# Fused attention and feed-forward: queries transposed a group sooner, half-width output tiles, one attention tile fewer

## The chip, the cores and the metric

The kernel runs on one core of a Trainium2 chip. A core has TensorE (PE, matmuls; its weight loads are listed apart as PEld), VectorE (DVE), ScalarE (ACT), GpSimd (POOL) and SyncE (SP), which run their own instruction streams and wait for each other through semaphores. SP, ACT and POOL also issue DMA transfers, which share 16 DMA engines. The metric is the device time of one execution in microseconds; lower is better. Everything below that has a time in it comes from the runs of the kernel, from the profile page of one profiled execution, or from queries of the trace of that execution. Line numbers (L309) are those of the kernel before the change.

## The reference

Two layers run one after the other on 8 batches, 12 heads, 448 positions and 64 dimensions per head:

```python
scores = (q @ k.transpose(0, 1, 3, 2)) / sqrt(64)
attn   = maximum(scores, 0) ** 2 / 448
x      = (attn @ v)  # heads side by side: 8 x 448 x 768
xn     = (x - mean(x)) / sqrt(var(x) + 1e-6) * g_ln
out    = x + maximum(xn @ w_ch1, 0) @ w_ch2   # w_ch1 768 x 3072, w_ch2 3072 x 768
```

There is no softmax: a score is squared after a Relu, so a product with the values needs no row sum. Inputs and output are float32; the kernel multiplies in bfloat16.

## The kernel before

**Groups.** The work of attention is cut into 24 groups (`groups`), three per batch, numbered 0 to 23; a group holds four heads (two rows `r` of two heads `hh`). For each group the kernel needs queries and keys transposed, with the head dimension on the partitions. In batches 0 and 1 PE makes these transposes. From group 6 on (`by_dma * G`) DMA transposes do, issued by SP: one for the keys of a group (`keys_dma`, L256, into a `kT` tile, of which there are three) and two for its queries (`queries_dma`, L261 and L262, into a `qT` tile, of which there are two). The sources come by loads that POOL issues (`load`, L120): the queries of a group into one of three fixed buffers (`qbuf`), its keys into one of three `k` tiles, its values into one of four.

**Scores and products.** For each of a group's seven key blocks `scores` does four small matmuls into a PSUM tile of the pool `ps_sc` (three tiles, L309), lets ACT write the Relu into a tile of the pool `apool` (ten tiles, L320) and DVE square it in place (L322). When the seven tiles of a group are there, `values` multiplies them with the values: 28 matmuls into another `ps_sc` tile (L339), in this order, where tile `i` and row `r` follow from `divmod(pr * J + j, 2)` with `J = 7`:

```python
for j in range(J):
    for hh in range(2):
        for pr in range(2):
            i, r = g["where"](pr, j)   # reads g["attn"][i]
```

DVE writes the product as `xT` and, times the norm's weight, as `xc`; POOL sums `xT` for the mean.

**Feed-forward.** `ffn1` multiplies `xc` with the first weights into `hT` (L525, 24 blocks of 448 columns per batch). `ffn2` multiplies `hT` with the second weights (L563): for each of 7 token tiles of 128 rows per pair of batches and each half of 384 columns, 24 matmuls into a bank of the pool `ps_mm` (two banks). The normalization's scale and the residual come afterwards: DVE multiplies the bank with `rstd` and adds `xtok`, the tokens of the pair transposed back by one long DMA transpose (`tokens`, L497), and writes the result into `o_sb` (L569). An `o_sb` tile has both halves, 768 columns; there are two. After the second half SP issues two stores of 64 rows each (L578). The very last token tile (`ffn2_last`) is cut into three pieces, one of 384 and two of 192 columns, each stored by itself from SP and from ACT (L599).

**The order.** The schedule is manual: each engine runs its instructions in the order in which the program text issues them, and the tile pools only add waits. Four pairs of batches pass through. While `ffn2` of one pair runs, the attention of the next pair is woven in (`interleave`): `attention` makes bundles of three score tiles, and after a bundle's item with `i` of 1 or 2 comes the product of the group before. After the last score tile of a group n comes a step, `transposed(n + 2)`, which issues on POOL the loads of keys n+5 and queries n+4 and on SP the two query transposes of n+2 and the key transpose of n+3. The stores of `ffn2` stand in the same SP queue. Between two such stages lie about 55 us of `ffn1` alone. Group 6 is transposed at the end of batch 1's attention, and group 7 by a step of its own right after `tokens(0)`.

The names that the change touches: `opool`, `apool`, the `qT` tiles, `keys_dma`, `queries_dma`, `transposed`, `item` in `attention`, `ffn2`, `ffn2_last`, and the call of `transposed` after `tokens(0)`.

Of the kernel before, what the change touches and what calls it, by code (L numbers as in the profile page):

```python
# [9 lines left out]
ALU = mybir.AluOpType  # L10
# [18 lines left out]
def kernel(  # L29
# [32 lines left out]
    J = S // HP  # L62
# [14 lines left out]
    wpool = ctx.enter_context(tc.tile_pool(name="w", bufs=1))  # L77
    io = ctx.enter_context(tc.tile_pool(name="io", bufs=4))
    tpool = ctx.enter_context(tc.tile_pool(name="t", bufs=2))
    apool = ctx.enter_context(tc.tile_pool(name="attn", bufs=10))  # L80
    xpool = ctx.enter_context(tc.tile_pool(name="x", bufs=1))
    xcpool = ctx.enter_context(tc.tile_pool(name="xc", bufs=2))
    xtpool = ctx.enter_context(tc.tile_pool(name="xt", bufs=1))
    hpool = ctx.enter_context(tc.tile_pool(name="h", bufs=1))
    opool = ctx.enter_context(tc.tile_pool(name="o", bufs=2))
    spool = ctx.enter_context(tc.tile_pool(name="stat", bufs=2))
    ps_sc = ctx.enter_context(tc.tile_pool(name="ps_sc", bufs=3, space=bass.MemoryType.PSUM))
    ps_mm = ctx.enter_context(tc.tile_pool(name="ps_mm", bufs=2, space=bass.MemoryType.PSUM))
# [19 lines left out]
    def load(n, names):  # L108
        if n >= len(groups):
            return  # L110
        b, m = groups[n]
        for name in names:
            if b == 1 and name != "v":
                o = (2 * m + "qk".index(name)) * 2 * S
                t = hold[:, o:o + 2 * S].rearrange("p (r s) -> p r s", r=2)
            elif name == "q":
                t = qbuf[m][:, D:D + 2 * S].rearrange("p (r s) -> p r s", r=2)
            else:
                t = io.tile([P, 2, S], bf16, tag=name, name=name + "_sb", bufs=4 if name == "v" else 3)
            nc.gpsimd.dma_start(t, srcs[name][b][:, m:NP:G, :])  # L120
            qkv[name, b, m] = t
# [90 lines left out]
    def transposes(b, m):  # L212


        if b == 0:
            o = 12 * 1024 + m * 2 * J * P
            sb = early[:, o:o + 2 * J * P].rearrange("p (i c) -> p i c", c=P)
        elif m:
            o = (m - 1) * 2 * J * P
            sb = hold[:, o:o + 2 * J * P].rearrange("p (i c) -> p i c", c=P)  # L220
        else:
            sb = tpool.tile([P, NB, P], bf16, tag="qT", name="qT_sb")
        dve, act = nc.vector.tensor_copy, nc.scalar.copy
        if (b, m) == (0, 0):

            cast(dve, "q", 0, 3)
            cast(act, "k", 0, 3)
            cast(act, "k", 3, J)
            idle(30)
            piece(sb, b, m, "q", ((dve, 0, 3),))  # L230
            idle(2)
            piece(sb, b, m, "k", ((dve, 0, 3), (dve, 3, J)))
            idle(3)
        elif b == 0:
# [15 lines left out]
    kts = {}  # L250

    def keys_dma(n):
        if n >= len(groups):
            return
        kts[n] = tpool.tile([P, J, P], bf16, tag="kT", name="kT_sb", bufs=3)
        nc.sync.dma_start_transpose(kts[n], qkv[("k",) + groups[n]].rearrange("p r s -> p (r s)"))  # L256

    def queries_dma(n):
        m, kt = groups[n][1], kts[n]
        qt = tpool.tile([P, NB, P], bf16, tag="qT", name="qT_sb")  # L260
        nc.sync.dma_start_transpose(qt[:, 0:2 * J + 1:2, :], qbuf[m][:, :])  # L261
        nc.sync.dma_start_transpose(qt[:, 1:2 * J:2, :], qbuf[m][:, D:D + 2 * S])  # L262

        def queries(i, r):
            o = (2 * i + r) // J * J + 1 - r
            return qt[:, o:o + J]
        st[groups[n]] = {
            "q": queries,
            "k": lambda i: kt[:, i],
            "where": lambda pr, j: divmod(pr * J + j, 2),  # L270
            "attn": []}
# [127 lines left out]
    def transposed(n):  # L399

        if groups[n][0] < by_dma:
            transposes(*groups[n])
            return


        if n == by_dma * G:
            keys_dma(n)
        else:
            if n == by_dma * G + 1:
                load(n + 2, "k")  # L410
            load(n + 3, "k")
            load(n + 2, "q")
        queries_dma(n)
        keys_dma(n + 1)

    def attention_block(b, blk):

# [36 lines left out]
    def attention(bs):  # L454

        lo, hi = bs[0] * G, (bs[-1] + 1) * G
        seq = [(n, i) for n in range(lo, hi) for i in range(J)]

        def item(n, i):
            scores(n, (i,), FULL)
            if i == J - 1 and n + 2 < len(groups):
                transposed(n + 2)

        def product(n):
            values(n, FULL)  # L470
            load(n + 4, "v")

        def bundle(items, at):
            for o, it in enumerate(items):
                item(*it)
                if o == at:
                    product(it[0] - 1)
        units, due = [], [[], []]
        for s in range(0, len(seq), 3):
            items = seq[s:s + 3]  # L480
            at = max((o for o, (n, i) in enumerate(items[:2]) if n > lo and i in (1, 2)), default=-1)
            units.append(lambda items=items, at=at: bundle(items, at))
# [67 lines left out]
        nc.scalar.activation(hT[pair][:, 0, o:o + w], one, ACTF.Relu)  # L550
        nc.scalar.activation(hT[pair][:, 1:3, o:o + w], two, ACTF.Relu)

    o_sb = {}

    def ffn2(pair, t, half, part, parts=4):
        if half == 0 and part == 0:
            o_sb[t] = opool.tile([P, d_model], fp32, tag="o", name="o_sb")
        if part == 0:
            o_sb["ps"] = ps_mm.tile([P, 512], fp32, tag="mm", name="o_ps")
        ps, cols = o_sb["ps"], slice(half * DH, (half + 1) * DH)  # L560
        n = K2 // parts
        for ki in range(part * n, (part + 1) * n):
            nc.tensor.matmul(  # L563
                ps[:, :DH], hT[pair][:, ki, t * P:(t + 1) * P], w2[:, ki, cols],
                start=(ki == 0), stop=(ki == K2 - 1))
        if part < parts - 1:
            return
        heads = slice(half * HP, (half + 1) * HP)
        nc.vector.scalar_tensor_tensor(  # L569
            o_sb[t][:, cols].rearrange("p (c d) -> p c d", d=D),  # L570
            ps[:, :DH].rearrange("p (c d) -> p c d", d=D),
            rstd[pair][:, t:t + 1], xtok[pair][:, :, t, heads],
            op0=ALU.mult, op1=ALU.add)
        if half == 1:
            for u in range(2):
                b, j = divmod(2 * t + u, J)
                rows = out[2 * pair + b].rearrange("(p j) d -> j p d", j=J)[j]
                nc.sync.dma_start(rows, o_sb[t][u * HP:(u + 1) * HP, :])  # L578

    def ffn2_last(pair, t):  # L580

        o = opool.tile([P, d_model], fp32, tag="o", name="o_sb")
        for half, lo, hi in ((0, 0, K1), (1, 0, G), (1, G, K1)):
            cols = slice(half * DH + lo * D, half * DH + hi * D)
            w = (hi - lo) * D
            ps = ps_mm.tile([P, 512], fp32, tag="mm", name="o_ps")
            for ki in range(K2):
                nc.tensor.matmul(  # L588
                    ps[:, :w], hT[pair][:, ki, t * P:(t + 1) * P], w2[:, ki, cols],
                    start=(ki == 0), stop=(ki == K2 - 1))  # L590
            nc.vector.scalar_tensor_tensor(  # L591
                o[:, cols].rearrange("p (c d) -> p c d", d=D),
                ps[:, :w].rearrange("p (c d) -> p c d", d=D),
                rstd[pair][:, t:t + 1], xtok[pair][:, lo:hi, t, half * HP:(half + 1) * HP],
                op0=ALU.mult, op1=ALU.add)
            for u, queue in enumerate((nc.sync, nc.scalar)):
                b, j = divmod(2 * t + u, J)
                rows = out[2 * pair + b].rearrange("(p j) d -> j p d", j=J)[j]
                queue.dma_start(rows[:, cols], o[u * HP:(u + 1) * HP, cols])  # L599

    def ffn1_units(b, blk=FULL):
        if blk == FULL:
# [35 lines left out]
    interleave(ffn1_units(1, BLK[1][0]), attention_block(1, BLK[1][1]), 3, 1)  # L638
    tokens(0)
    transposed(by_dma * G + 1)  # L640
    for unit in ffn1_units(1, BLK[1][1]):
        unit()
    statistics(0, 0)
# [42 lines left out]
```

## Time and profile before

| What | us |
|---|---|
| median of 3 runs (551.58 to 556.33) | 552.45 |
| profiled execution, its own time | 551.32 |
| its span, from the first to the last instruction | 549.5 |
| PE busy in the span | 538.7 |
| DVE, ACT, POOL busy | 266.0, 260.2, 109.2 |
| attention woven into output, first, second and third time | 102 to 176, 231 to 307, 362 to 436 |
| output of the last pair alone | 491 to 549.5 |

| Transfer | Issued by | Count | Issue to landing, median us |
|---|---|---|---|
| queries transposed, L261 and L262 | SP | 36 | 6.8 |
| keys transposed, L256 | SP | 18 | 5.2 |
| tokens transposed, L497 | SP | 4 | 12.3 |
| output, 192 KB each, L578 | SP | 54 | 3.6 |
| queries loaded, 224 KB each, L120 | POOL | 20 | 7.7 |
| keys loaded, 224 KB each, L120 | POOL | 20 | 7.2 |

A timeline row has the start, the length (of the whole run of instructions, where it merges several), the engine, the line, what is written and read, and in brackets the idle time before it and what ended that. A row with SPq is the issue of a transfer, not the transfer: SP can be held there while the DMA queues are full. The landing is the time of the semaphore update. In the rows by stage, the DMA share adds up the queues' packets over 16 engines and can pass 1 where two queues overlap.

### The profile page before, as it was taken

The page shows a single profiled execution, that of the slowest core. Times are in us where ns is not written, and L with a number is a line of the kernel's source. Part 1 is how long each engine was busy: PE and PEld are TensorE (multiplying, and loading weights), DVE is VectorE, ACT ScalarE, POOL GpSimd, SP SyncE. Part 2 cuts the span into 40 slices and gives each one's busy share as a digit, 9 for nine tenths or more (in the row PEclk, how much of TensorE's full clock was granted, in tenths as well). Part 3 has the DMA queues.
Part 4 walks back from the last instruction along what each step waited for, and adds up shares of the span by engine and source line. Part 5 has one row for each costly group of instructions (what it writes and reads, how often), then busy time and mean ns, then how long its engine had stood idle before and what let it go on. Part 6 is the DMA issues. An engine that isn't in the chain of part 4 may idle for free.

```text
span 549.5 us, 10988 instructions
## 1 busy us (share of the span) xinstructions
PE 538.7 (98%) x4734; PEld 318.3 (58%) x4734; DVE 266.0 (48%) x511; ACT 260.2 (47%) x424; POOL 109.2 (20%) x135
## 2 busy tenths in 40 slices
PE   7899999999999999999999999999999999999997
PEld 5687779655555555555555555555555555555655
DVE  4776753378886250057777532027687670001111
ACT  5776775455553444455545344445545244440000
POOL 7334102024426100003614400001230400000000
PEclk8999999999999999999999999999999999999999
DMA  9999999979999900028999960006941250001222
GB/s 188 207 204 208 210 194 148 117 116 162 164 176 127 212 2 1 0 59 144 123 142 160 173 124 1 0 1 91 170 102 30 60 100 0 1 0 30 58 57 58
DMA packets 107216, 56.62 MB, mean 103 GB/s; under 512 B 77216, under 2 KB 103712, under 8 KB 107168
## 3 DMA queue, kind: packets, MB, share of 16 engines
q1 hardware_dynamic: 79680, 29.77, 32.3%
q0 software_dynamic: 26976, 25.50, 31.7%
q8 instruction: 37, 0.61, 0.5%
q10 hardware_dynamic: 512, 0.66, 0.3%
q14 instruction: 11, 0.09, 0.1%
HBM read 51.91 MB, written 11.01 MB: 115 GB/s over the span
## 4 chain that ended last, share of the span: by engine, by line
PE 90%; DMA 8%; issue 0%; POOL 0%; DVE 0%; SPq 0%; POOLq 0%
PE o_ps L563 38%; PE h_ps L525 38%; PE sc_ps L309 6%; DMA w<-in_moe_w_ch_dram 5%; PE av_ps L339 5%; DMA qT_sb<-q_sb 2%; PE o_ps L588 1%; DMA q_sb<-in_q_dram 1%; PE h_ps L547 1%; PE sum_ps L387 1%; PE tr_ps L205 0%; POOL k_sb L120 0%; POOL q_sb L120 0%; DVE o_sb L591 0%; POOL identity masks.py:199 0%
## 5 line engine op out<-in xcount | busy, mean ns | idle before, releaser
L525 PE MATMUL h_ps<-xc_sb,w 128*128 128x448 bf16 (+2 forms) x1368 | 219.2, 318 | 0.6 <-DVE hT_sb L531 0.4
L563 PE MATMUL o_ps<-w,hT_sb 128*128 128x384 bf16 x1296 | 219.6, 326 | 0.0
L525 PEld LDWEIGHTS <-w 128*128 128x128 bf16 x1368 | 128.6, 98 | 86.9 <-issue 3.1
L563 PEld LDWEIGHTS <-hT_sb 128*128 128x128 bf16 x1296 | 123.1, 98 | 94.2 <-issue 16.0
L320 ACT ACTIVATE attn_sb<-sc_ps 128x896 bf16<-128x896 f32 (+4 forms) x150 | 126.4, 902 | 84.6 <-PE sc_ps L309 84.6
L533 ACT ACTIVATE hT_sb<-h_ps 128x448 bf16<-128x448 f32 (+2 forms) x212 | 102.5, 483 | 121.5 <-PE h_ps L525 121.1
L322 DVE TENSOR_TENSOR attn_sb<-attn_sb 128x896 bf16<-128x896 bf16 x126 | 81.5, 654 | 39.1 <-ACT attn_sb L320 38.2
L569 DVE SCALAR_TENSOR_TENSOR o_sb<-o_ps,rstd_sb,xtok_sb 128x384 f32<-128x384 f32 x54 | 33.0, 611 | 49.1 <-PE o_ps L563 48.7
L510 DVE RECIPROCAL rstd_sb<-rstd_sb 128x1 f32<-128x1 f32 (+1 forms) x10 | 1.7, 168 | 98.0 <-ACT rstd_sb L509 98.0
L504 DVE BATCH_NORM_STATS2 stats<-xtok_sb 128x6 f32<-128x384 bf16 x56 | 27.5, 533 | 32.7 <-DMA xtok_sb<-xT_sb 32.7
L370 POOL TENSOR_TENSOR part_sb<-part_sb,xT_sb 128x448 f32<-128x448 f32 x24 | 29.5, 1229 | 66.9 <-DVE xT_sb L346 59.3
L367 POOL TENSOR_TENSOR part_sb<-xT_sb 128x448 f32<-128x448 bf16 x6 | 6.6, 1106 | 168.6 <-DVE xT_sb L346 138.7
L393 DVE SCALAR_TENSOR_TENSOR xc_sb<-total_sb,g_mean,xc_sb 128x448 bf16<-128x448 f32 (+2 forms) x54 | 29.0, 605 | 21.2 <-ACT total_sb L391 21.2
L309 PE MATMUL sc_ps<-qT_sb,kT_sb 64*64 64x448 bf16 x504 | 34.7, 357 | 1.5 <-DMA qT_sb<-q_sb 1.5
L339 PE MATMUL av_ps<-attn_sb,v_sb 64*64 64x448 bf16 (+2 forms) x672 | 32.3, 327 | 0.0
L346 DVE TENSOR_SCALAR xT_sb<-av_ps 128x896 bf16<-128x896 f32 (+2 forms) x30 | 26.9, 900 | 9.4 <-PE av_ps L339 9.4
L352 DVE TENSOR_SCALAR xc_sb<-xT_sb,g_sb 128x448 bf16<-128x448 bf16 (+2 forms) x56 | 28.6, 558 | 1.0
L339 PEld LDWEIGHTS <-v_sb 64*64 64x64 bf16 x840 | 22.9, 107 | 10.6 <-issue 1.6
L120 POOL DMA_DIRECT2D k_sb<-in_k_dram x20 | 14.2, 713 | 47.0 <-DMA kT_sb<-k_sb 37.0
L309 PEld LDWEIGHTS <-kT_sb 64*64 64x64 bf16 x504 | 11.5, 105 | 18.5 <-issue 15.0
L120 POOL DMA_DIRECT2D v_sb<-in_v_dram x24 | 17.4, 729 | 21.7 <-PE av_ps L339 17.9
L320 ACT ACTIVATE early<-sc_ps 128x768 bf16<-128x768 f32 (+3 forms) x24 | 18.3, 827 | 2.7 <-PE sc_ps L309 2.5
(63 smaller groups left out, 196.1 us busy)
## 6 DMA issues: line engine op xcount, KB each, us to landing
out_dram<-o_sb SPq DMA_DIRECT2D x54, 192.0 KB, 3.6
v_sb<-in_v_dram POOLq DMA_DIRECT2D x24, 224.0 KB, 4.9
w<-in_moe_w_ch_dram POOLq DMA_DIRECT2D x12, 384.0 KB, 14.5
w<-in_moe_w_ch_dram POOLq DMA_DIRECT2D x4, 1152.0 KB, 20.0
q_sb<-in_q_dram POOLq DMA_DIRECT2D x20, 224.0 KB, 7.7
k_sb<-in_k_dram POOLq DMA_DIRECT2D x20, 224.0 KB, 7.2
hold_sb<-in_q_dram POOLq DMA_DIRECT2D x3, 224.0 KB, 11.9
hold_sb<-in_k_dram POOLq DMA_DIRECT2D x3, 224.0 KB, 11.1
```

Of the source, the lines that this page charges most:

```text
L120: nc.gpsimd.dma_start(t, srcs[name][b][:, m:NP:G, :])
L309: nc.tensor.matmul(ps[cols, r, o * w:(o + 1) * w], g["k"](i)[rows, cols], g["q"](i, r)[rows, blk[0]:sum(blk), cols], start=True, stop=True)
L320: nc.scalar.activation(a, ps[:, :, :len(slots) * w], ACTF.Relu)
L322: nc.vector.tensor_mul(a, a, a)
L339: nc.tensor.matmul(ps[cols, hh, :w], v_sb[rows, pr, j * D:(j + 1) * D], g["attn"][i][rows, r, :], start=(j == 0), stop=(j == J - 1))
L352: nc.vector.tensor_scalar_mul(xc[b][:, c, of(blk)], xT[b // 2][:, c, of(blk, b)], g_sb[:, c:c + 1])
L370: nc.gpsimd.tensor_add(part[b], part[b], x[:, c])
L393: nc.vector.scalar_tensor_tensor(xc[b][:, c, of(blk)], total, g_mean[:, c:c + 1], xc[b][:, c, of(blk)], op0=ALU.mult, op1=ALU.add)
L525: nc.tensor.matmul(ps[:, :w], w1[:, c, ni * P:(ni + 1) * P], xc[b][:, c, of(blk)], start=(c == 0), stop=(c == K1 - 1))
L533: nc.scalar.activation(hT[pair][:, ni, o:o + w], ps[:, :w], ACTF.Relu)
L563: nc.tensor.matmul(ps[:, :DH], hT[pair][:, ki, t * P:(t + 1) * P], w2[:, ki, cols], start=(ki == 0), stop=(ki == K2 - 1))
L569: nc.vector.scalar_tensor_tensor(o_sb[t][:, cols].rearrange("p (c d) -> p c d", d=D), ps[:, :DH].rearrange("p (c d) -> p c d", d=D), rstd[ ...
```

## The change

- The `qT` tiles get three buffers. The step after group n issues the transposes of group n+3, keys first, then the two for the queries; before, it issued the queries of n+2 and then the keys of n+3. The loads of a step are the keys and queries of one group, n+5; before, the keys of n+5 and the queries of n+4. There is one more call, for group 8, after `tokens(0)`; the keys of group 7 come after the token transpose, where they stood ahead of it.
- An output tile has 384 columns, and there are three of them; before, two of 768. Each half is stored after its own eviction, with two stores of 64 rows, so the stores are twice as many with half the bytes each. The last token tile goes through the same function, and its three pieces have a tile each.
- The pool of attention tiles has nine, before ten.

The instructions of PE, ACT and DVE and their order stay the same; what the waits name, and the queues of SP and POOL, change.

```diff
-    apool = ctx.enter_context(tc.tile_pool(name="attn", bufs=10))
+    apool = ctx.enter_context(tc.tile_pool(name="attn", bufs=9))
...
-    opool = ctx.enter_context(tc.tile_pool(name="o", bufs=2))
+    opool = ctx.enter_context(tc.tile_pool(name="o", bufs=3))
...
     def keys_dma(n):
-        if n >= len(groups):
-            return
...
     def queries_dma(n):
         m, kt = groups[n][1], kts[n]
-        qt = tpool.tile([P, NB, P], bf16, tag="qT", name="qT_sb")
+        qt = tpool.tile([P, NB, P], bf16, tag="qT", name="qT_sb", bufs=3)
...
-        if n == by_dma * G:
-            keys_dma(n)
-        else:
-            if n == by_dma * G + 1:
-                load(n + 2, "k")
-            load(n + 3, "k")
-            load(n + 2, "q")
+        if n > by_dma * G:
+            load(n + 2, "kq")
+        keys_dma(n)
         queries_dma(n)
-        keys_dma(n + 1)
...
         def item(n, i):
             scores(n, (i,), FULL)
-            if i == J - 1 and n + 2 < len(groups):
-                transposed(n + 2)
+            if i == J - 1 and n + 3 < len(groups):
+                transposed(n + 3)
...
         if part < parts - 1:
             return
-        heads = slice(half * HP, (half + 1) * HP)
-        nc.vector.scalar_tensor_tensor(
-            o_sb[t][:, cols].rearrange("p (c d) -> p c d", d=D),
-            ps[:, :DH].rearrange("p (c d) -> p c d", d=D),
-            rstd[pair][:, t:t + 1], xtok[pair][:, :, t, heads],
-            op0=ALU.mult, op1=ALU.add)
-        if half == 1:
-            for u in range(2):
-                b, j = divmod(2 * t + u, J)
-                rows = out[2 * pair + b].rearrange("(p j) d -> j p d", j=J)[j]
-                nc.sync.dma_start(rows, o_sb[t][u * HP:(u + 1) * HP, :])
+        finish(pair, t, half, 0, K1, ps, (nc.sync, nc.sync))
+
+    def finish(pair, t, half, lo, hi, ps, queues):
+
+        cols, w = slice(half * DH + lo * D, half * DH + hi * D), (hi - lo) * D
+        o = opool.tile([P, DH], fp32, tag="o", name="o_sb")
+        nc.vector.scalar_tensor_tensor(
+            o[:, :w].rearrange("p (c d) -> p c d", d=D),
+            ps[:, :w].rearrange("p (c d) -> p c d", d=D),
+            rstd[pair][:, t:t + 1], xtok[pair][:, lo:hi, t, half * HP:(half + 1) * HP],
+            op0=ALU.mult, op1=ALU.add)
+        for u, queue in enumerate(queues):
+            b, j = divmod(2 * t + u, J)
+            rows = out[2 * pair + b].rearrange("(p j) d -> j p d", j=J)[j]
+            queue.dma_start(rows[:, cols], o[u * HP:(u + 1) * HP, :w])
...
     tokens(0)
     transposed(by_dma * G + 1)
+    transposed(by_dma * G + 2)
```

More of the change, by code (lines that the diff above doesn't have):

```diff
@@ L221, in transposes @@
         else:
-            sb = tpool.tile([P, NB, P], bf16, tag="qT", name="qT_sb")
+            sb = tpool.tile([P, NB, P], bf16, tag="qT", name="qT_sb", bufs=3)
         dve, act = nc.vector.tensor_copy, nc.scalar.copy
@@ L551, in ffn1_head @@
         nc.scalar.activation(hT[pair][:, 1:3, o:o + w], two, ACTF.Relu)
-    o_sb = {}
+    acc = [None]
     def ffn2(pair, t, half, part, parts=4):
-        if half == 0 and part == 0:
-            o_sb[t] = opool.tile([P, d_model], fp32, tag="o", name="o_sb")
         if part == 0:
-            o_sb["ps"] = ps_mm.tile([P, 512], fp32, tag="mm", name="o_ps")
-        ps, cols = o_sb["ps"], slice(half * DH, (half + 1) * DH)
+            acc[0] = ps_mm.tile([P, 512], fp32, tag="mm", name="o_ps")
+        ps, cols = acc[0], slice(half * DH, (half + 1) * DH)
         n = K2 // parts
@@ L567, in ffn2 @@
             return
-        heads = slice(half * HP, (half + 1) * HP)
+        finish(pair, t, half, 0, K1, ps, (nc.sync, nc.sync))
+    def finish(pair, t, half, lo, hi, ps, queues):
+        cols, w = slice(half * DH + lo * D, half * DH + hi * D), (hi - lo) * D
+        o = opool.tile([P, DH], fp32, tag="o", name="o_sb")
         nc.vector.scalar_tensor_tensor(
-            o_sb[t][:, cols].rearrange("p (c d) -> p c d", d=D),
-            ps[:, :DH].rearrange("p (c d) -> p c d", d=D),
-            rstd[pair][:, t:t + 1], xtok[pair][:, :, t, heads],
+            o[:, :w].rearrange("p (c d) -> p c d", d=D),
+            ps[:, :w].rearrange("p (c d) -> p c d", d=D),
+            rstd[pair][:, t:t + 1], xtok[pair][:, lo:hi, t, half * HP:(half + 1) * HP],
             op0=ALU.mult, op1=ALU.add)
-        if half == 1:
-            for u in range(2):
-                b, j = divmod(2 * t + u, J)
-                rows = out[2 * pair + b].rearrange("(p j) d -> j p d", j=J)[j]
-                nc.sync.dma_start(rows, o_sb[t][u * HP:(u + 1) * HP, :])
+        for u, queue in enumerate(queues):
+            b, j = divmod(2 * t + u, J)
+            rows = out[2 * pair + b].rearrange("(p j) d -> j p d", j=J)[j]
+            queue.dma_start(rows[:, cols], o[u * HP:(u + 1) * HP, :w])
     def ffn2_last(pair, t):
-        o = opool.tile([P, d_model], fp32, tag="o", name="o_sb")
         for half, lo, hi in ((0, 0, K1), (1, 0, G), (1, G, K1)):
-            cols = slice(half * DH + lo * D, half * DH + hi * D)
-            w = (hi - lo) * D
+            cols, w = slice(half * DH + lo * D, half * DH + hi * D), (hi - lo) * D
             ps = ps_mm.tile([P, 512], fp32, tag="mm", name="o_ps")
@@ L590, in ffn2_last @@
                     start=(ki == 0), stop=(ki == K2 - 1))
-            nc.vector.scalar_tensor_tensor(
-                o[:, cols].rearrange("p (c d) -> p c d", d=D),
-                ps[:, :w].rearrange("p (c d) -> p c d", d=D),
-                rstd[pair][:, t:t + 1], xtok[pair][:, lo:hi, t, half * HP:(half + 1) * HP],
-                op0=ALU.mult, op1=ALU.add)
[L596 to L599, printed above, removed]
+            finish(pair, t, half, lo, hi, ps, (nc.sync, nc.scalar))
     def ffn1_units(b, blk=FULL):
```

## The prediction

> **What bounds the kernel now.** I read the page's busy line first, then the busy time by stage, then who waited for whom on TensorE (PE), then the timeline around the one wait found, and last the issue queue of SyncE (SP) there.
>
> ```profile
> span 549.5 us, 10988 instructions
> PE 538.7 (98%) x4734; PEld 318.3 (58%) x4734; DVE 266.0 (48%) x511; ACT 260.2 (47%) x424; POOL 109.2 (20%) x135
> ```
>
> By stage (length, then busy us of PE, PEld, DVE, ACT and POOL, PE clock, DMA share, GB/s):
>
> ```profile
> 0.00:42.00 42.00, 36.70 (x636) 28.39 (x638) 27.39 (x74) 28.80 (x51) 21.79 (x37) 0.96 1.18 200
> 102.00:176.00 74.00, 74.00 (x674) 40.12 (x673) 59.15 (x108) 37.76 (x50) 25.86 (x29) 1.00 0.96 147
> 231.00:307.00 76.00, 74.52 (x675) 40.36 (x674) 52.05 (x81) 37.18 (x45) 24.54 (x27) 1.00 0.88 124
> 362.00:436.00 74.00, 74.00 (x673) 40.12 (x672) 52.11 (x80) 36.93 (x45) 15.63 (x15) 1.00 0.45 78
> 491.00:549.50 58.50, 54.52 (x360) 34.22 (x357) 9.07 (x16) 0.63 (x2) 0.00 (x0) 1.00 0.19 48
> ```
>
> PE stands idle for 549.5 - 538.7 = 10.8 us: 5.3 at the start (weights still loading), 4.0 at the end (last eviction and store), and 1.48 between, all of it in the second attention stage, 231 to 307. The first and third attention stages have no idle time at all. So the change, which touches the attention and output stages, can win 1.5 us and not much more, and it loses only what it makes PE wait.
>
> The Trainium skill ("Trainium Kernel Development and Optimization", Performance Expectations) warns that matmul busy time is a bad measure, since matmuls overlap, and would have one look at weight loads, here 58%; by that a large reserve could hide in the 98%. The row decides otherwise: successive 384-column matmuls of L563 start 162.5 ns apart (124.009, 124.171, 124.334), and that page's 2.4 GHz makes 160 ns of 384 columns.
>
> The one wait, in the timeline:
>
> ```profile
> 263.55 2.32 SPq L261 DMA_TRANSPOSE qT_sb<-q_sb  x1
> 265.92 2.99 SPq L262 DMA_TRANSPOSE qT_sb<-q_sb  x1
> 269.01 4.86 SPq L256 DMA_TRANSPOSE kT_sb<-k_sb  x1
> ...
> 274.07 0.38 PE L309 MATMUL sc_ps<-qT_sb,kT_sb 64*64 64x448 bf16 x4
> ...
> 275.26 1.11 SPq L578 DMA_DIRECT2D out_dram<-o_sb  x2
> ...
> 275.94 0.57 PE L309 MATMUL sc_ps<-qT_sb,kT_sb 64*64 64x448 bf16 x8 [1.48 <-DMA qT_sb<-q_sb]
> ```
>
> Group 16's query transposes are issued at 263.55 and 265.92, after the last scores of group 14; the second lands at 275.80, 9.9 us later, and group 16 begins there instead of at 274.46. Set beside each group's first scores, the other landings are early, but some barely: group 9 by 1.5 us (134.65 against 136.19), group 10 by 0.9, group 17 by 0.3 (288.97 against 289.25). The groups come about 10 us apart, and the landings of query transposes range from 3.1 to 11.4 us: the lead of one group is just too short where the DMA share is near or over 1.
>
> **The change, part by part.**
>
> 1. *Queries a group sooner, with their keys.* The step after group n now issues keys and queries of n+3; before it issued queries of n+2 and keys of n+3. The number of transposes per step (three), of loads (one k, one q) and their order on the engines PE, ACT and DVE are the same. The lead of a query transpose grows by a group, some 10 us, so the 1.48 us goes: **-1.5**. What is late next? Keys have that lead already, and no wait for keys is in PE's list; the worst step above lasted from 263.55 to the keys' landing at 276.49, 13 us, where the new lead is 20. The third buffer is what allows it: queries n+3 overwrite those of n, whose scores have just been issued, as with two buffers before.
>
> On POOL the load of queries n+5 now waits for the transposes of n+2, issued a step before, as the load of keys did already; POOL spent 37 us in such key waits with nothing late for it, and the sums behind (L370) waited for DVE, not for POOL.
>
> At the start there is one more step: after the token transpose of pair 0 come keys and queries of 7, then of 8. Keys 7 used to be issued at 80.28, ahead of the token transpose, which holds SP from 85.68 to 97.13; now they come after. Queries 7 were issued from 97.13 to 104.23 and landed at 107.81; with 1.3 us of keys ahead, 109.1; group 7 begins at 113.2: 4 us to spare. Group 8 follows on SP to about 110, lands by about 116 (queries had a median of 6.8 us), and begins at 123.2. **0**; with the longest landing of any, 11.4 us from a start near 101, still 112.4 and 0. If this cover goes, PE waits once, for the excess.
>
> 2. *Half tiles out.* DVE's 57 evictions are the same instructions. 54 stores of 192 KB become 108 of 96 KB. SP gets 54 more issues of 0.53 us (the pairs take 1.11): 28.6 us over the span, 1.1 us per group. In the worst step SP has no idle time from 262.34 to 273.87, so the transposes behind can slip 1.1 us per step, over the four such steps (263 to 306) 4.4 us: less than the 10 us gained. The three half buffers give a store the time of three halves: half 0 evicted at 271.58 would be issued when SP is free, at 273.9 to 275, land by 281.5 (the stores' longest landing is 7.5 from issue), and its buffer is wanted at about 285. DVE doesn't wait; and behind DVE PE has a second o_ps bank, half a tile or 3.9 us of matmuls, more with scores between. **0**. The tail: the last pieces have the same sizes and queues as before (1.9 to 2.4 us to landing), and the buffer of the last was stored 7.8 us earlier. **0**.
>
> The Trainium skill speaks against this part ("DMA: Bandwidth & Descriptors", Rules for kernel authors: coalesce small transfers, under 64 KB they are mostly overhead; Anatomy of one DMA gives 2.0 us fixed plus bytes/436e3). By its formula alone, 54 more stores would be 108 us of fixed cost if nothing overlapped it. The trace's 96 and 48 KB stores at the end landed in 1.9 to 2.4 us, which agrees with the fixed part, but nothing waits there for a store except the program's end.
>
> 3. *Nine attention tiles.* Ten were alive where the product of group n-1 is issued after score tile 2 of group n (four times per pair: products of its groups 0, 1, 3, 4). Now the Relu of tile 2 must wait until the product has read tile 0 of the old group. The product runs over j outermost, then hh, then pr; tile 0 holds the blocks j=0 and j=1 of pr=0, so its last reader is the 7th of 28 matmuls. The places where two scores follow the product in the same bundle matter (products 0 and 3 of a pair; 6 in all), since the third then needs the scores' bank of tile 2:
>
> ```profile
> 283.75 0.38 PE L309 MATMUL sc_ps<-qT_sb,kT_sb 64*64 64x448 bf16 x4
> 283.96 1.49 PE L339 MATMUL av_ps<-attn_sb,v_sb 64*64 64x448 bf16 x28
> 284.18 0.92 ACT L320 ACTIVATE attn_sb<-sc_ps 128x896 bf16<-128x896 f32 x1 [2.67 <-PE sc_ps L309]
> ...
> 285.29 0.55 PE L309 MATMUL sc_ps<-qT_sb,kT_sb 64*64 64x448 bf16 x8
> ```
>
> The 7th matmul ends at 284.51 and the scores at 284.13: the Relu starts 0.38 us later, ends near 285.48 instead of 285.10, and tile 4's scores start at 285.48 now. With a handover of 0.05 us (scores' end 284.132 to Relu's start 284.184) PE loses about 0.05 us; with that of the two PE waits on ACT's L320 that the trace has (0.7 us in 2), 0.35. I take 0.1, nearer the direct handover: **+0.6** for six; bounds 0 and 2.1. In the other six places scores of tile 1 are still in ACT's queue until after the 7th matmul: 0. In batch 1's blocks at most eight tiles are alive: 0.
>
> **Sum**: -1.5 + 0 + 0 + 0.6 = -0.9 us. The profiled execution took 551.32 us (span 549.5, 1.8 around it), so **550.4**. The runs' median, 552.45, lies 1.1 above the profiled one; landings that were early by 0.3, 0.9 and 1.5 us may have been late in those, and this is what a longer lead also removes, so I stay at 550.4 and not at 551.5.
>
> **The rivals.**
>
> *A. The gain is eaten* (551.3 to 552.6). The handover costs 0.25 to 0.35 us in each of the six places, 1.5 to 2.1 us, or the transposes were not what made the runs differ. For: PE must be woken within 0.1 us. Against: the Relu starts 0.05 us behind its scores everywhere.
>
> *B. Slower: the Relu waits for the whole product.* If tile 0 is let go only when all 28 matmuls have ended (285.457), the Relu ends at 286.43 and tile 4's scores lose 0.95 us, six times 5.7, less the 1.5: +4.2, **555.5**. It decides from a release later than the 7th matmul by more than 0.1 us. Against: the order of reads above.
>
> *C. Slower: halves slow a full DMA queue.* 3,456 more packets at the hardware queue's mean (32.3% of 16 engines over 549.5 us for 79,680 packets: 36 ns) are 7.7 us of all sixteen engines, 2.8 of it in the 20 halves or so of the two dense stretches; if transposes are that much later and the lead doesn't cover it, -1.5 + 0.6 + 2.8: **553.2**. It decides only once a step's backlog passes 20 us.
>
> *D. A clean gain* (549.0 to 549.9): handover free, and nothing lost.
>
> **How the numbers follow.** Forecast (549.9 to 551.3) 0.50; A 0.19; B 0.08; C 0.08; D 0.10; B and C together, or a stall on SP that I don't see, beyond 558: 0.05. The range, 549.0 to 554.0, holds the forecast, A, D and C. A measurement here can tell about 1% from no change: faster than 546.9 would need half of all PE's idle time, 0.02; within 1% 0.91; above 558 0.07 (the 0.05, and a part of B).
>
> **What would show it.** Right: no wait of PE for qT_sb; the second attention stage full on PE at 75 to 76 us; in the six places a Relu that starts 0.8 us after its scores do, not 0.43 (283.75 to 284.18); PE busy near 538.7. Wrong: PE waiting for ACT's L320 by more than 0.1 us a place, DVE waiting for out_dram stores, PE waiting for kT_sb or qT_sb at 113 or 123 us, or a longer span with PE idle in the first or third attention stage, where there is none now.

## The result and the profile after

| Kernel | Runs | Median us | Lowest to highest us |
|---|---|---|---|
| before | 14 | 552.96 | 550.77 to 556.33 |
| after | 14 | 549.52 | 549.19 to 552.40 |

The ratio after to before is 0.9946, with a 95% interval of 0.9926 to 0.9966: faster by half a per cent, some 3 us. The forecast was 550.4 us, 0.9 below the profiled execution of before; the median came 1.8 below that execution. Which terms the other 0.9 us belong to is worked out below.

The first profiled execution of the changed kernel took 552.11 us and had a span of 550.3 us, more than the 549.5 of before. It isn't typical, and one row says why. This is the first stage of it (stretch, length, busy us of PE, PEld, DVE, ACT and POOL, granted clock, DMA share, GB/s):

```profile
0.00:42.00 42.00, 36.05 (x598) 27.43 (x599) 25.98 (x70) 27.29 (x47) 20.72 (x35) 0.88 1.18 199
```

The clock granted to PE was 0.88 in the first 42 us on average (it stood at 0.50 from 8 to 17 us), 0.96 in the profile of before. In a second profiled execution of the same kernel (run e3 below, 550.08 us) it was 1.00. The first place where the schedule has scores, product and scores in a row starts at 120.05 us in the one and at 118.04 in the other; these 2.0 us are the whole difference of the two executions (552.11 and 550.08). So the profile shown from here on is that of e3. Its page and its stages, in the order in which those of before were read:

```profile
span 548.3 us, 11108 instructions
PE 539.3 (98%) x4734; PEld 318.9 (58%) x4734; DVE 266.3 (49%) x511; ACT 260.1 (47%) x424; POOL 109.5 (20%) x135
...
q0 software_dynamic: 26976, 25.50, 31.8%
q1 hardware_dynamic: 84000, 29.77, 30.4%
```

```profile
0.00:42.00 42.00, 36.57 (x620) 28.38 (x622) 26.99 (x73) 28.47 (x50) 21.70 (x37) 1.00 1.18 200
102.00:176.00 74.00, 74.00 (x673) 40.18 (x672) 58.27 (x105) 38.09 (x51) 26.69 (x31) 1.00 0.99 152
231.00:307.00 76.00, 76.00 (x684) 41.28 (x682) 52.51 (x81) 37.22 (x45) 25.41 (x28) 1.00 0.84 128
362.00:436.00 74.00, 74.00 (x673) 40.12 (x671) 52.53 (x80) 36.49 (x43) 15.68 (x15) 1.00 0.38 72
491.00:548.30 57.30, 53.71 (x355) 33.67 (x352) 8.92 (x16) 0.00 (x0) 0.00 (x0) 1.00 0.20 49
```

The second attention stage, 74.52 us busy on PE before, is now full: 76.00 of 76. The list of waits has no line for `qT_sb` or `kT_sb`; as the three attention stages are full, none of what is left is in them, and DVE's one wait for a store is 0.2 us. Here are the first three lines of PE and that of DVE (us in total, times, longest):

```profile
PE tr_ps L205 <- DVE q_sb L158: 1.3, 1, 1.3
PE idle_ps L191 <- DVE ones L93: 1.1, 1, 1.1
PE sc_ps L307 <- ACT early L318: 1.0, 2, 0.7
...
DVE o_sb L565 <- DMA out_dram<-o_sb: 0.2, 1, 0.2
```

The timeline where group 16 waited before, SP first, then PE:

```profile
266.20 4.16 SPq L259 DMA_TRANSPOSE qT_sb<-q_sb  x1
270.41 2.89 SPq L260 DMA_TRANSPOSE qT_sb<-q_sb  x1
273.39 3.62 SPq L573 DMA_DIRECT2D out_dram<-o_sb  x4
```

```profile
274.73 0.76 PE L307 MATMUL sc_ps<-qT_sb,kT_sb 64*64 64x448 bf16 x12
```

The transposes are no faster to issue: SP still stands 7 us over a pair. But they are those of group 17; group 16's had landed at 263.70, 11 us ahead of its first scores. The bundle of twelve (four of group 15, eight of group 16), which was torn at 274.46 before, runs in one piece.

**A ledger by landmarks.** The matmuls of PE are the same in both kernels, so I set the profiles side by side by the starts of the six places of step 3, each the start of the four score matmuls just ahead of a product (283.75 in the prediction is the fourth):

| Stretch, us | before | after (e3) | difference |
|---|---|---|---|
| span's start to place 1 | 117.61 | 118.04 | +0.43 |
| place 1 to place 6 | 295.32 | 294.01 | -1.31 |
| place 6 to the last landing of a store | 135.19 | 135.26 | +0.07 |
| last landing to the span's end | 1.35 | 0.98 | -0.37 |
| span | 549.47 | 548.30 | -1.17 |

The first row varies by itself (117.3 to 118.7 in the profiles of the runs below, whatever the kernel). The second is the subject of the experiments: it holds both the wait and the cost of the nine tiles, and in a kernel with neither it is 293.65 (run e4). The last row I had not expected.

### The profile page after: what moved, and what is told of

It is laid out like the page before. It is cut to its first block, busy times and chain, and to the rows that moved or that the text cites. A ratio compares the mean times of both kernels' runs of the same rounds, so it can differ in the third digit from the quotient of the medians.

```text
span 550.3 us, 11108 instructions
## 1 busy us (share of the span) xinstructions
PE 540.8 (98%) x4734; PEld 320.1 (58%) x4734; DVE 266.4 (48%) x511; ACT 260.4 (47%) x424; POOL 109.5 (20%) x135
## 3 DMA queue, kind: packets, MB, share of 16 engines
q0 software_dynamic: 26976, 25.50, 32.3%
## 4 chain that ended last, share of the span: by engine, by line
PE 96%; DMA 2%; ACT 1%; DVE 1%; SPq 0%; issue 0%; DVEq 0%
PE o_ps L554 39%; PE h_ps L518 39%; PE sc_ps L307 7%; PE av_ps L337 6%; DMA g_sb<-in_moe_g_ln_dram 2%; PE o_ps L581 1%; PE h_ps L540 1%; PE sum_ps L385 1%; PE tr_ps L205 1%; ACT early L318 1%; DVE early L296 0%; ACT early L209 0%; SPq L177 0%; ACT xc_sb L348 0%; DVE early L209 0%; DVE hT_sb L524 0%
## 5 line engine op out<-in xcount | busy, mean ns | idle before, releaser
L565 DVE SCALAR_TENSOR_TENSOR o_sb<-o_ps,rstd_sb,xtok_sb 128x384 f32<-128x384 f32 (+1 forms) x57 | 34.4, 604 | 56.4 <-PE o_ps L554 49.8
L497 DVE BATCH_NORM_STATS2 stats<-xtok_sb 128x6 f32<-128x384 bf16 x56 | 27.5, 533 | 30.4 <-DMA xtok_sb<-xT_sb 30.4
L337 PE MATMUL av_ps<-attn_sb,v_sb 64*64 64x448 bf16 (+2 forms) x672 | 32.3, 327 | 0.0
L337 PEld LDWEIGHTS <-v_sb 64*64 64x64 bf16 x840 | 23.3, 109 | 10.3 <-issue 1.3
L307 PEld LDWEIGHTS <-kT_sb 64*64 64x64 bf16 x504 | 12.1, 105 | 17.6 <-issue 13.3
```

The costliest lines, as they stand in the source:

```text
L307: nc.tensor.matmul(ps[cols, r, o * w:(o + 1) * w], g["k"](i)[rows, cols], g["q"](i, r)[rows, blk[0]:sum(blk), cols], start=True, stop=True)
L337: nc.tensor.matmul(ps[cols, hh, :w], v_sb[rows, pr, j * D:(j + 1) * D], g["attn"][i][rows, r, :], start=(j == 0), stop=(j == J - 1))
L565: nc.vector.scalar_tensor_tensor(o[:, :w].rearrange("p (c d) -> p c d", d=D), ps[:, :w].rearrange("p (c d) -> p c d", d=D), rstd[pair][:, ...
```

## The experiments

Theory W: the gain is PE's wait for query transposes, which in many runs is longer than the 1.48 us of the profile, and the longer lead removes it. Rivals: K, the clock granted at the start; H, the half tiles do it. Then, for what makes the transposes late: F, the bytes that the stores put right ahead of them; S, the packet size of the stores; L, the loads that POOL issues in the same step. Each ratio is to the kernel before on the same chip.

### Set 1: which part, and is it the wait

Before: 551.53 us median of 28 runs (550.48 to 555.7).

**e1, no edit: the kernel before.**

> The kernel before, unchanged, for its spread and a second profile. Theory W (the gain is PE's wait for query transposes, which differs from one execution to the next): runs spread over several us, 550.8 to 556, at a TensorE clock that doesn't explain it (0.99 to 1.00), and in the profile the waits of TensorE for qT_sb add up to the run's time less about 549.5. Rival K (the runs differ by the granted clock at the start): times follow the clock, and the waits for qT_sb stay at 1.5 us.

Measured: 551.9 us (550.63 to 557.05, 12 runs), ratio 1.0008 (0.9981 to 1.0035). Its profile has the start at full clock and a longer wait than the first (the wait, then the first 42 us and the second attention stage):

```profile
PE sc_ps L309 <- DMA qT_sb<-q_sb: 2.6, 1, 2.6
```

```profile
0.00:42.00 42.00, 36.95 (x640) 28.80 (x642) 27.73 (x75) 28.80 (x51) 21.89 (x37) 1.00 1.18 200
231.00:307.00 76.00, 73.45 (x670) 39.68 (x668) 51.62 (x80) 37.06 (x45) 23.68 (x26) 1.00 0.83 122
```

The same kernel in another execution loses 2.55 us at the same group 16 where the first lost 1.48, and place 1 to place 6 takes 296.40 us. What the run has above 549.5, 2.75 us, is what this stretch lost against 293.65, as W asked. With the start at 1.00 it still takes 552.25 us, so K can't be the whole of it. The other half of the expectation, a spread that the clock doesn't explain, failed: the five of the 12 runs above 553 us have a mean granted clock of 0.991 to 0.995, the other seven (550.63 to 552.25 us) 0.999 or 1.000.

**e2, all of the change but the queries:** two `qT` buffers and the old step; half tiles and nine attention tiles stay.

```diff
-    opool = ctx.enter_context(tc.tile_pool(name="o", bufs=2))
+    opool = ctx.enter_context(tc.tile_pool(name="o", bufs=3))
-    apool = ctx.enter_context(tc.tile_pool(name="attn", bufs=10))
+    apool = ctx.enter_context(tc.tile_pool(name="attn", bufs=9))
     # ffn2, finish, ffn2_last as in the change; transposed() as before
```

> The changed kernel with the old step (queries of n+2, then keys of n+3, two query buffers, loads as before): half tiles and nine attention tiles stay. Theory W: no gain, within 0.3% of the kernel before (552 to 554), with waits for qT_sb in the profile. Rival H (half tiles bring the gain, by smaller bursts and by freeing SP sooner): 549.5, as the changed kernel.

Measured: 549.98 us (549.44 to 552.64, 12 runs), ratio 0.9964 (0.9946 to 0.9982). The wait at group 16 is still there, but 0.2 us long (place 1 to place 6 takes 294.45 us, 0.44 more than in the changed kernel):

```profile
PE sc_ps L309 <- DMA qT_sb<-q_sb: 0.2, 1, 0.2
```

That W alone makes the gain is refuted: without the lead, most of it is there. What is missing is the certainty: 4 of the 12 runs are above 550.5.

**e3, no edit: the changed kernel.**

> The changed kernel again, for a profile at full clock and its per-run clocks. Both theories: 549.3 to 549.8, no wait for qT_sb; runs at a mean clock near 0.991 come at 552. Rival K: the difference to the kernel before vanishes between runs of equal clock.

Measured: 549.51 us (549.36 to 550.1, 9 runs), ratio 0.9959 (0.9942 to 0.9976); the profile shown above.

**e4, before without the wait:** the scores of groups 6 to 23 read the key tile where they read the query tile. The query transposes are still issued, and nobody reads them.

```diff
         def queries(i, r):
             o = (2 * i + r) // J * J + 1 - r
-            return qt[:, o:o + J]
+            return kt[:, 0:J]
```

> The kernel before, in which the scores of groups 6 on read the transposed keys in place of the transposed queries, so the result is another; all query transposes are still issued, but nobody reads them. Full tiles and ten attention tiles. Theory W: TensorE loses no time in attention, 549.2 to 549.8, narrow spread, as the changed kernel less its handover cost (0 to 0.6). Rival H: stays at 552 to 553.5. Rival K: stays as spread out as the kernel before.

Measured: 549.63 us (549.12 to 552.24, 8 runs, the other seven up to 550.13), ratio 0.996 (0.994 to 0.998). Full tiles, ten attention tiles, all transfers, and only the wait gone: the gain is there. Place 1 to place 6 takes 293.65 us. Against this, before had lost 1.67 us in its first profile and 2.75 in e1, mostly the waits of 1.48 and 2.55 that the lists show. So the wait is what the change gains from, whichever part shortens it.

**The granted clocks of the runs.** In the 96 runs of before in the three sets, the median is 551.34 us at a mean clock of 0.999 and above (31 runs) and 553.97 below 0.995 (21 runs). In the runs of the changed kernel (the result, e3 and e12) it is 549.55 (21 runs) and 552.11 (3 runs). At equal clock some 1.8 us remain, near what e4 gives, so K isn't the gain. But K has a share in the spread: 36 of the 38 runs of before above 553 us have a clock below 0.999. Below 0.995 the changed kernel, which has no such wait, loses about as much. Between 0.995 and 0.998 it doesn't (549.48 in 11 runs, 551.57 at most), while 17 of 44 runs of before are above 553; why these are isn't shown. The 14 runs of before in the result have no clock on record, so how much of the 3.4 us between those two medians is the clock stays open.

### Set 2: why half tiles alone shorten it

Before: 552.77 us median of 33 runs (550.7 to 557.11).

**e5, before with half tiles alone** (`opool` with three half buffers, `ffn2` and `ffn2_last` through `finish`; ten attention tiles, old step).

```diff
-    opool = ctx.enter_context(tc.tile_pool(name="o", bufs=2))
+    opool = ctx.enter_context(tc.tile_pool(name="o", bufs=3))
     # ffn2, finish, ffn2_last as in the change
```

> The kernel before with half tiles alone (old step, two query buffers, ten attention tiles). After e2, theory F: half tiles let the queries land sooner, because half of a token tile's bytes have left before the step, so only 192 KB and not 384 KB stand right ahead of the query transposes in SP's queue. Then 549.2 to 550.2 median, with waits for qT_sb of 0 to 1 us; 0.4 under e2, the six handovers of 0.07 us that nine tiles cost. If instead the nine tiles had been what helped: 551.5 to 553.

Measured: 549.99 us (549.2 to 553.64, 11 runs), ratio 0.996 (0.9932 to 0.9987). Place 1 to place 6: 294.26, that is 0.61 lost in place of 1.67 to 2.75. Groups 16 and 17 begin 0.1 us after their second query transpose landed, so the margin is nil, and 4 of the 11 runs are above 550.8.

**e6, half tiles whose stores are all issued after the second half.**

```diff
+        held.append(store)
+        if half == 1 or queues[1] is nc.scalar:
+            for s in held:
+                s()
+            held.clear()
```

> Half tiles as in e5, but the stores of both halves are issued together after the second half, so that again 384 KB (in four stores) stand right ahead of the step. Theory F: the gain is gone, 551.5 to 553, waits for qT_sb of 1.5 us and more, in group 16. Rival S (the smaller size alone helps): as e5, 549.2 to 550.2.

Measured: 549.89 us (549.17 to 552.65, 11 runs), ratio 0.9949 (0.9923 to 0.9974), place 1 to place 6 294.35. PE still waits 0.5 us at group 16. This run was no test of F: a store of the first half waits only for its own half, and as SP had nothing in between, it issued them at 261.31 and 261.90, right behind the key transpose, as in e5 (260.44 and 261.04, with all of that schedule 1.3 us sooner). Run e9 holds them back.

**e7, before without the stores of the first three pairs** (42 of the 54 stores are left out, so most of the output isn't written).

```diff
-        if half == 1:
+        if half == 1 and pair == B // 2 - 1:
```

> The kernel before without the stores of the first three pairs (that part of the output is not written). Theory F: the queries land early enough everywhere, no wait for qT_sb, 549.2 to 549.8, and group 16's second query transpose lands 1.5 to 3 us earlier after the step's start than the 12.3 us of before. If stores have no part in it: the wait stays and so does 551.5 to 553.

Measured: 550.62 us (548.91 to 553.98, 10 runs), ratio 0.996 (0.9931 to 0.9988). With no store at all in the stage the wait is still 0.9 us:

```profile
PE sc_ps L309 <- DMA qT_sb<-q_sb: 0.9, 1, 0.9
```

So the stores aren't the cause: the second query transpose of group 16 still lands 11.5 us after its issue. They may be a part of the crowd, as the median is 2.15 us lower; of that, 0.37 is the shorter end of the program, described below. Nor is the kernel faster without these stores than with the half tiles (549.99). (Place 1 to place 6: 295.06; 0.33 of the loss lies at group 10 and 1.07 at group 16.)

**e8, before without the loads of queries, keys and values from group 9 on** (these groups compute with the rows of the batch before).

```diff
         for name in names:
+            if n >= 9:
+                qkv[name, b, m] = qkv[name, b - 1, m]
+                continue
```

> The kernel before without the loads of queries, keys and values from group 9 on (the three older groups' data are used again, so the result is another). If POOL's loads are the other half of the crowding: query transposes land 4 to 6 us after their issue in the stage from 231 to 307, not 6 to 12, no wait for qT_sb, 549.2 to 549.8. If the transposes are slow by themselves: landings stay near 7 us median and the wait stays.

Measured: 549.43 us (549.22 to 550.18, 10 runs), ratio 0.9943 (0.9918 to 0.9968), place 1 to place 6 293.65, no wait. The same step of SP:

```profile
263.21 1.30 SPq L264 DMA_TRANSPOSE qT_sb<-q_sb  x1
264.56 1.42 SPq L265 DMA_TRANSPOSE qT_sb<-q_sb  x1
266.02 1.85 SPq L259 DMA_TRANSPOSE kT_sb<-k_sb  x1
```

It takes SP 4.7 us where it took 10.3 (263.55 to 273.87), and the two query transposes land 5.2 and 4.7 us after their issue; before it was 11.3 and 9.9. The median landing of a query transpose is 3.6 us, before 6.8. What crowds the transposes are the loads beside them.

### Set 3: packets against bytes, and the loads themselves

Before: 551.57 us median of 35 runs (550.34 to 555.7).

**e9, full tiles stored with four stores of 64x384,** the second half's first, so that SP holds all four back until the tile is whole.

```diff
-                nc.sync.dma_start(rows, o_sb[t][u * HP:(u + 1) * HP, :])
+                nc.sync.dma_start(rows[:, DH:], o_sb[t][u * HP:(u + 1) * HP, DH:])
+            for u in range(2):
+                b, j = divmod(2 * t + u, J)
+                rows = out[2 * pair + b].rearrange("(p j) d -> j p d", j=J)[j]
+                nc.sync.dma_start(rows[:, :DH], o_sb[t][u * HP:(u + 1) * HP, :DH])
```

> Before with one edit: full output tiles, but four stores of 64x384 instead of two of 64x768, all issued after the second half, so the same 384 KB go out at once, in the packets of the half tiles. Theory F (half tiles help because the bytes ahead of group 16's transposes are half): as before, 551 to 553 us, and PE waits for group 16's query transposes by 1 us or more. Rival S (the smaller packets help): about 549.9 us and a wait below 0.5 us.

Measured: 550.33 us (549.14 to 552.45, 12 runs), ratio 0.997 (0.9948 to 0.9991). Place 1 to place 6: 294.22. The 0.57 us lost are at group 10; the second attention stage is full:

```profile
PE sc_ps L309 <- DMA qT_sb<-q_sb: 0.4, 1, 0.4
```

```profile
102.00:176.00 74.00, 73.63 (x671) 39.83 (x669) 58.84 (x107) 38.21 (x51) 24.94 (x28) 1.00 1.00 143
231.00:307.00 76.00, 76.00 (x685) 41.20 (x683) 52.52 (x81) 37.43 (x46) 25.17 (x28) 1.00 0.78 127
```

F's wait of 1 us at group 16 isn't there: the same bytes in one go, and most of the gain of the half tiles. S fits, but isn't shown. Of the 1.24 us between the medians 0.37 is the shorter end of the program, and at a clock of 0.999 and above they are 0.67 us apart (550.31 in 9 runs, 550.98 in 12). Something else moved besides the packets: the two further stores hold SP, so that the transposes go out 1.3 us later after the loads beside them (263.83 and 264.54) than before. And e7, with no store packets at all in the stage, kept the wait. Group 16's transposes, issued 2.2 us later than before (265.78), landed 8.1 and 7.4 us after their issue. How smaller store packets could let them by sooner isn't shown either: packets of transposes took 30 ns on average before and 29 here, no clear difference, while packets of stores went from 175 ns (3072 bytes) to about 89 (1536 bytes).

**e10, before with the loads later:** the loads of keys and queries that a step issues move on POOL's queue behind the first sum (L370) of the next product.

```diff
+    def late_loads(n):
+        if n >= by_dma * G:
+            load(n + 5, "k")
+            load(n + 4, "q")
...
+                if c == 2 * m:
+                    late_loads(b * G + m)
...
-            load(n + 3, "k")
-            load(n + 2, "q")
+                load(n + 3, "k")
+                load(n + 2, "q")
```

> Before with one edit: the loads of keys n+3 and queries n+2 that the step after group n issues on POOL's queue are issued later, behind the first sum of product n; the transposes of the step keep their place, two query buffers, full tiles and ten attention tiles stay. Theory L (the query transposes are late because the step's own loads move beside them): 549.1 to 549.8 us, hardly a spread, no wait of PE for qT_sb, and the query transposes of group 16 land within 7 us. Rival (whatever moves at that time crowds them, the loads no more than the rest): 551 to 553 us and a wait of 1 us or more at group 16, or a wait for kT_sb or qT_sb elsewhere.

Measured: 549.76 us (549.37 to 551.01, 12 runs), ratio 0.9958 (0.9939 to 0.9978), no wait for `qT_sb` or `kT_sb`, place 1 to place 6 293.65. The loads at group 16's transposes before:

```profile
262.15 0.74 POOL L120 DMA_DIRECT2D v_sb<-in_v_dram  x1
262.88 0.72 POOL L120 DMA_DIRECT2D k_sb<-in_k_dram  x1
263.59 0.73 POOL L120 DMA_DIRECT2D q_sb<-in_q_dram  x1
```

And here, with the transposes between loads at 261.59, 263.31 and then 270.60:

```profile
261.59 0.72 POOL L120 DMA_DIRECT2D q_sb<-in_q_dram  x1
...
263.31 0.74 POOL L120 DMA_DIRECT2D v_sb<-in_v_dram  x1
263.81 2.28 SPq L261 DMA_TRANSPOSE qT_sb<-q_sb  x1
...
266.14 2.92 SPq L262 DMA_TRANSPOSE qT_sb<-q_sb  x1
...
269.15 1.52 SPq L256 DMA_TRANSPOSE kT_sb<-k_sb  x1
270.60 0.74 POOL L120 DMA_DIRECT2D k_sb<-in_k_dram  x1
```

The two loads that stood at 262.88 and 263.59 have moved to 270.60 and later; those of the step before, moved likewise, now stand here, at 260.86 and 261.59, some 2 us sooner. So the crowd is spread out, not taken away. The transposes landed after 8.8 and 7.2 us, not within the 7 us expected, but 1.2 us ahead of their scores. So the wait goes with the full output tiles, two query buffers and ten attention tiles of before, by moving two loads. L holds in kind; the margin is thin.

**e11, the late loads and the half tiles together,** ten attention tiles, two query buffers (the edits of e5 and e10).

> The late loads of the run before together with the half tiles of the change, ten attention tiles and two query buffers kept. Theory L, with the ten tiles' cheaper handover (0.43 us over six places): 549.0 to 549.4 us, 0.2 to 0.5 below the changed kernel. Rival: as the changed kernel or behind it, 549.5 to 550, with a wait for qT_sb left in some runs.

**e12, no edit: the changed kernel beside it.**

> The changed kernel again, beside the three others on the same chip: 549.3 to 549.7 us by every theory, ratio to before 0.993 to 0.997.

Measured: e11 549.31 us (548.85 to 550.7, 12 runs), ratio 0.9952 (0.9932 to 0.9972); e12 549.62 us (549.23 to 552.47, 12 runs), ratio 0.9972 (0.9953 to 0.999). Place 1 to place 6: 293.65 and 294.01. The 0.36 us between them is what nine attention tiles cost in these five places. The medians differ by 0.31; as the two intervals overlap, the runs alone don't settle that e11 is faster, the trace says why it should be. Its margin at group 16 is 2.5 us, that of the changed kernel 12.1.

## Why the prediction was right, and where it was not

The time fell inside the range, but in the band of rival D (549.0 to 549.9), 0.9 below the forecast; D's reason, a handover at no cost, is not what happened. By the steps:

1. **Queries a group sooner, -1.5: right in kind, too small.** No wait for `qT_sb` is left in any profile of the changed kernel, and the margins of groups 7 to 17 are 7.8 us and more. The size was one execution's: place 1 to place 6 lost 1.67 us in that profile, 2.75 in e1, and with nothing else changed (e4) the medians differ by 1.9 us. The prediction said that the landings early by 0.3, 0.9 and 1.5 us could be late in other runs, and then stayed at the profile's number. It should have counted them: group 10, early by 0.9, was late in e7 and e9. The 1.1 us by which the runs' median lay above the profile was a possible sign, though the clock at the start moves runs as well. Runs of before up to 557 us remain without a profile; nearly all above 553 have a lowered clock, and how much of their excess is wait isn't shown.
2. **The step at the start, 0: right.** In e3 group 7's queries landed at 105.46, 8.1 us before its first scores, and group 8's at 110.74, 12.8 us before; I had allowed 109.1 and 116.
3. **Half tiles, 0: right that they cost nothing, wrong that they bring nothing.** Alone they gave 0.996 (e5). Two things were missed: half tiles shorten the wait by themselves (place 1 to place 6 loses 0.61 us in e5; 1.67 and 2.75 before), for a reason that e6, e7 and e9 leave open, and the program's end is 0.37 us shorter, of which more below. Since the longer lead removes the same wait, the two gains don't add up: e2 549.98, e5 549.99, the whole change 549.5. DVE's wait of 0.2 us is as good as the none I expected, and the two stores that SP issued at 273.39 and 273.99 had landed by 276.17 (allowed for such a pair: 281.5). The rule of the Trainium skill that spoke against this part ("DMA: Bandwidth & Descriptors", Rules for kernel authors: coalesce small transfers) puts its line at 64 KB, and the halves have 96 KB; its formula, in Anatomy of one DMA, is for transfers that GpSimd issues, and SP issues these. No cost of splitting showed here: the same bytes in twice the stores (e9) gave 0.997.
4. **Nine attention tiles, +0.6: right in kind, 0.43 in size.** The fourth place in the changed kernel, PE and then ACT:

```profile
282.73 0.38 PE L307 MATMUL sc_ps<-qT_sb,kT_sb 64*64 64x448 bf16 x4
282.94 1.50 PE L337 MATMUL av_ps<-attn_sb,v_sb 64*64 64x448 bf16 x28
284.26 0.62 PE L307 MATMUL sc_ps<-qT_sb,kT_sb 64*64 64x448 bf16 x8
284.82 0.34 PE L554 MATMUL o_ps<-w,hT_sb 128*128 128x384 bf16 x1
```

```profile
283.53 0.92 ACT L318 ACTIVATE attn_sb<-sc_ps 128x896 bf16<-128x896 f32 x1 [3.04 <-PE av_ps L337]
```

ACT's Relu now waits for the product (`av_ps`) and starts 0.80 us after the scores; I had said 0.8, against 0.43. The next `o_ps` matmul comes 2.09 us after the scores, 2.02 before: 0.07 us a place, in all six places alike, 0.43 together. In place of the 0.1 that I took, the lower end of my 0.05 to 0.35 was near.

The sum in its own terms, from the profile of before: -1.67 + 0 - 0.37 + 0.43 = -1.6, or 549.7 us from the profiled 551.32; the median was 549.52; the last 0.2 us I can't assign. PE was busy for 539.3 us, where I had said near 538.7.

**The rivals.** A (gain eaten) fell with the handover's 0.07 us. B (the Relu waits for the whole product) fell at the same row: 283.53 lies in the middle of the product, 282.94 to 284.44. C had a wrong price: 36 ns a packet was the mean of a queue that mixes small and large ones. The queue's line shows it: q1 has 4,320 packets more (84000, before 79680; 3,456 for the halves and 16 for each of the 54 further stores), and its share of the engines went down, from 32.3 to 30.4%. The stores' packets took 37.7 us of each engine before (3,456 at 175 ns) and about 40.0 in e3 (6,912 at 93 ns, the other packets of 1536 bytes taken as before): 2.3 us over the whole program, not 7.7.

## What to carry to other kernels

- A wait that one profile shows at 1.5 us, with neighbours that are early by less than 1, is a sample of a distribution. Its price is the distance of the runs from a kernel that can't wait, at equal granted clock, and the cheapest way to learn that is to make the reader read something else (e4: 1.9 us, at all clocks and at 0.999 and above alike).
- When a transfer is late, look at what is issued beside it before giving it more buffers: here moving two loads behind one sum won as much as a third buffer and a longer lead, though with less margin.
- Count a mean price per packet only for packets of the same size.

## What was not expected of the hardware

- **The end of the program has a price that goes with the number of stores.** After the last landing SP still runs closing semaphore waits, 0.06 us each: eight in before (548.14 to 548.57), two in e3 (547.33 and 547.39). In all other kernels with the 60 stores of before there are eight as well (e1, e4, e8, e10; 1.34 to 1.36 us from the last landing to the span's end), in all with 114 (e2, e3, e5, e6, e9, e11, e12) or 18 (e7) two (0.97 to 0.99). The loads have no part in it: e8 has 45 fewer and still eight waits. That it is the position of the last store among the semaphores that SP goes through is my reading of this, not shown.
- **Query transposes land in 3.6 us without the loads of POOL and in 6.8 beside them** (medians of e8 and before), and SP's issue of three took 4.7 us in place of 10.3.
- **The granted clock of the first 42 us differs from execution to execution of one kernel:** 0.88 and 1.00 for the changed one, and 2.0 us of its time with it. In the slower one it stood at 0.50 from 8 to 17 us, and at 1.00 from 18 to 42 us. Set side by side, the first profiled executions of the two kernels (551.32 and 552.11 us) have the wrong sign.
